# Decay rows sent straight to DRAM, sums left in their banks, and side work respaced in a decay-attention and two-FFN kernel

## The chip, the cores and the metric

One core of a Trainium2 chip runs the whole program in one launch. The metric is the device time of that launch in microseconds; of the timed runs the median counts. The engines are TensorE (PE in the profile; its weight loads PEld), VectorE (DVE), ScalarE (ACT), GpSimd (POOL) and SyncE (SP), which here only issues DMAs. Each works through its own queue in order.

## What is computed

Attention of 32 heads (4 batches of 8, 576 positions, head size 64) with a causal mask and a decay, then two feed-forward layers over 2304 tokens (512 to 2048 to 512), all in float32:

```python
scores = scale * np.matmul(q, k.transpose(0, 1, 3, 2))
log_f = np.log(np.clip(f, 0.0001, 1.0))
cum = np.cumsum(log_f, axis=-1)
decay = cum[:, :, :, None] - cum[:, :, None, :]
scores = np.where(causal, -1e9, scores + decay)
attn = softmax(scores)                       # written out in the reference
x = np.matmul(attn, v)                       # heads side by side: 2304 x 512
h = x @ w_in;  x = (h * np.clip(h + 3.0, 0.0, 6.0) / 6.0) @ w_out       # first layer
h = x @ w_in2; out = (np.maximum(h, 0) + alpha * np.minimum(h, 0)) @ w_out2   # second layer
```

## The kernel before

**Precision.** A float32 value is split into a high part (a cast, `fp32r`) and a low part (the value minus the cast), and a product is made of three matmuls: high by high, high by low, low by high. So each operand needs a cast on ACT and a subtraction on POOL or DVE.

**Attention** (lines 278 to 605) runs in 144 units, nine for each pair of heads: four query blocks of the first head, one tail unit for both, four blocks of the second. Unit t's scores are made at step t, the exps one step on, transposes and evacuation (`evac`, L408, L413) five steps on, into `pt` tiles. The decay is added by the matmul itself: rows 64 to 67 of the operands q2 and k2 hold the cumulated logarithms `hl` (high and low part) and constants. For heads 0 and 1 `aug_rows` copies these rows from SBUF; for the others all rows are written to DRAM once (`aq_d`, `ak_d`; L520, L536) and `prep_head` fetches four rows for each head (L313, L314). `aq` is a tile in which POOL has scaled `hl` by 1 (L531 to 534) beside memset constants. `load_head` (L295) loads a head's q and k. Head 2 is prepared at unit 3 and first used at unit 9. The tiles of the prologue (pool `pro`: fl, zero, cum, ak, aq) are given up behind it, and the pool of the `pt` tiles is opened in their place.

**The FFNs** work in sets of (layer, group g of 256 hidden columns, pair p of 768 tokens). For each set the first product is done as seven block products (Strassen-Winograd; `product`, L689): products 1, 6, 7, 4 add up in PSUM bank A, 5 and 3 in C, 2 in B. Partial sums are copied to SBUF tiles `s` by ACT (`keep`, L705) and added on DVE (`add`, L708); each sum is activated (`activate`: `first` on ACT L663 or L666 and L668, `second` on DVE L674 or L677, `third` a cast L682 on ACT and the low part L683 on POOL, the tile `g`), and the set after it multiplies g by w_out (`piece`, L731, L733). The order is written out: `SEQ` gives one step for each product (a digit) and each piece (`q`), 15 steps a set in the first layer and 13 in the second; `later(d, fn)` puts work d steps on.

**Side work** is put at steps by tables of names and step numbers (`conversion`, `build`). `conv_ops` turns 64-bit weights into float32 words (m on ACT L137; f, s, j, g on DVE L140 to L153; raw words come by `fetch`, L117), sums them (S1 to S4, POOL L167) and splits them (h on ACT L181, l on POOL L185). For four groups of the second layer the float32 words are made early and kept in DRAM (c, p: store and load, L195, L197); `CONV_TURN` is their table. `build` makes the seven X blocks of a pair: adds (a, L237), casts (h, ACT L240), subtractions (l, L245, in turn on the engines of `subs`). The third pair's blocks are built in the set (g 7, p 0) of each layer, by the list `BUILD`; pair 1 of the second layer in the last set of the first. A tile of a pool has as many buffers as it says; a new use waits for the readers of the old one.

Of the kernel before, what the change touches and what calls it, by code (L numbers as in the profile page):

```python
# [21 lines left out]
def decay_attention_ffn2_kernel(ctx, tc, qk, v, f, wi1, wo1, wi2, wo2, alpha, out):  # L22
# [22 lines left out]
    DRAIN = {9 * NP + 3: 2, 9 * NP + 4: 2, 9 * NP + 6: 2, 9 * NP + 7: 2}  # L45
    CONV_ATT = "m0 15 f0 16 s0 17 j0 18 g0 19 m1 24 f1 25 s1 26 j1 27 g1 28 hb 33 lb 35 S1 42 S3 42 S2 44 S4 44 ha 51 la 53 hc 53 lc 60 hd 60 ld 62 m2 69 f2 70 s2 71 j2 72 g2 73 m3 78 f3 79 s3 80 j3 81 g3 82 ho0 78 lo0 80 ho1 87 lo1 89 wi0 90 wi1 93 wo0 99 wo1 102"
    CONV_ATT1 = "m0 108 f0 109 s0 110 j0 111 g0 112 m1 117 f1 118 s1 119 j1 120 g1 121 S1 143 S3 145 S2 146 ha 146 hc 146 hb 147 la 147 lc 147 lb 148 S4 149 hd 149 ld 150 m2 150 f2 151 s2 151 j2 152 g2 153"
# [3 lines left out]
    CONV_EVEN = "m0 0 f0 1 s0 2 j0 3.5 g0 5 m1 4 f1 6.5 s1 8 j1 9 g1 10 S1 11 S2 12 S3 12 hc 13 ha 13 lc 14 hb 14 la 15 lb 16 S4 17 m2 18 hd 18 f2 19 ld 19 s2 20 j2 21 m3 21 g2 22.5 f3 23 ho0 23 lo0 24 s3 24.5 j3 26 g3 27 ho1 28 lo1 29 wi0 40 wi1 43 wo0 46 wo1 48"  # L51
    CONV_TURN = "p0 0 p1 0 S1 6 S2 7 S3 7 hc 8 ha 8 lc 9 hb 9 la 10 lb 11 S4 12 hd 13 ld 14 p2 14 p3 15 ho0 24 lo0 25 ho1 26 lo1 27 wi0 40 wi1 43 wo0 46 wo1 48"
    BUILD_FIRST = "h0 l0 a3 h3 l3 h2 l2 a4 a6 h6 l6 h4 l4 h1 l1 a5 h5 l5"
    BUILD = "h0 2 l0 4 a3 6 h3 9 l3 11 h2 9 l2 11 a4 13 a6 15 h4 16 l4 18 h1 17 l1 19 h6 19 l6 21 a5 22 h5 26 l5 28"
    early = {}
# [200 lines left out]

    def build_ops(k, p, add, subs, even=None):
        adds, highs, lows = build_parts(k, p, add, subs)
        if even is not None:
            fns = [{"h": highs, "l": lows, "a": adds}[name[0]][int(name[1]), c]  # L260
                   for name in BUILD_FIRST.split() for c in range(KH)]
            return [(even[0] + i / even[1], fn) for i, fn in enumerate(fns)]
        return [(t, {"h": highs, "l": lows, "a": adds}[name[0]][int(name[1]), c])
                for name, t in table(BUILD) for c in range(KH)]

# [12 lines left out]
    def attention():  # L278
        with ExitStack() as ax:
# [207 lines left out]
            def aug_rows(a):  # L487
# [50 lines left out]
            px.close()
# [115 lines left out]
    def activate(s, gt, i, n, h, d):  # L654
        ff, g, p = s
        if n not in gt:
            gt[n] = {}
        hold = {}

        def first():  # L660
            t = P["tp"].tile([128, NB], F32, tag="t", name="t")
            if ff == 0:
                nc.scalar.activation(out=t, in_=h(), func=AF.Relu, bias=three, scale=1.0)  # L663
                hold["g"] = t
                return
# [13 lines left out]

        def third():  # L680
            gt[n][i] = P["gp"].tile([128, 2, NB], F32R, tag=f"g{n}", name=f"g{n}", bufs=3 - n)
            nc.scalar.copy(out=gt[n][i][:, 0], in_=hold["g"])  # L682
            nc.gpsimd.tensor_sub(out=gt[n][i][:, 1], in0=hold["g"], in1=gt[n][i][:, 0].bitcast(F32))  # L683

        later(d, first)
        later(d + 1, second)
        later(d + 1, third)

    def product(s, c, gt, k):  # L689
# [67 lines left out]
    def side_work(s):  # L757
# [7 lines left out]

        def build(k, pair, subs, add=nc.vector, even=None):
# [17 lines left out]
        if p == NPR - 1:  # L784
# [118 lines left out]
```

## Time and profile before

| | us |
|---|---|
| median of 3 runs | 1015.56 (1013.59 to 1016.53) |
| profiled execution | 1012.13 |
| its span | 1010.3 |
| PE busy in the span | 965.5 |
| DVE, ACT, POOL busy | 735.9, 589.1, 590.0 |
| mean granted TensorE clock | 0.995 |

The profile is one execution, recorded by the hardware. Attention fills the span up to about 215 us, the first layer goes on to about 625, the second to the end. Matmuls are pipelined and their ends are modelled, so a PE that is always busy need not be at its peak; a gap in it is a real gap. A mark `[3.86 <-DMA k<-ak_d]` behind a row means that the engine sat idle for 3.86 us before it and that this DMA ended the idle time. The granted clock is a share of 2.4 GHz.

### The profile page before, as it was taken

The page shows a single profiled execution, that of the slowest core. Times are in us where ns is not written, and L with a number is a line of the kernel's source. Part 1 is how long each engine was busy: PE and PEld are TensorE (multiplying, and loading weights), DVE is VectorE, ACT ScalarE, POOL GpSimd, SP SyncE. Part 2 cuts the span into 40 slices and gives each one's busy share as a digit, 9 for nine tenths or more (in the row PEclk, how much of TensorE's full clock was granted, in tenths as well). Part 3 has the DMA queues.
Part 4 walks back from the last instruction along what each step waited for, and adds up shares of the span by engine and source line. Part 5 has one row for each costly group of instructions (what it writes and reads, how often), then busy time and mean ns, then how long its engine had stood idle before and what let it go on. Part 6 is the DMA issues. An engine that isn't in the chain of part 4 may idle for free.

```text
span 1010.3 us, 15919 instructions
## 1 busy us (share of the span) xinstructions
PE 965.5 (96%) x5488; PEld 859.7 (85%) x5488; DVE 735.9 (73%) x1284; ACT 589.1 (58%) x1444; POOL 590.0 (58%) x577
## 2 busy tenths in 40 slices
PE   4999999999999999999999989999999999999998
PEld 3767666678899999998998988789898888898997
DVE  6888988857698788878989846145687788735454
ACT  5677787776555555555654445665565656564452
POOL 8567568956646666566485269566556556532222
PEclk9999999999999999999999999999999999999999
DMA  6555576501424444310576851332344420243531
GB/s 219 174 173 168 176 239 208 150 2 42 156 66 177 178 175 169 107 48 1 198 308 241 308 184 48 137 129 81 125 160 168 166 84 1 104 182 142 229 150 68
DMA packets 36868, 147.57 MB, mean 146 GB/s; under 512 B 4668, under 2 KB 4668, under 8 KB 33652
## 3 DMA queue, kind: packets, MB, share of 16 engines
q1 hardware_dynamic: 36784, 146.56, 41.7%
q8 instruction: 43, 0.70, 0.3%
q14 instruction: 37, 0.30, 0.1%
q10 hardware_dynamic: 4, 0.00, 0.0%
HBM read 98.26 MB, written 44.14 MB: 141 GB/s over the span
## 4 chain that ended last, share of the span: by engine, by line
PE 57%; DVE 23%; POOL 7%; ACT 6%; issue 4%; DMA 2%; SPq 0%; POOLq 0%; ACTq 0%; DVEq 0%
PE o L733 13%; PE hA L700 12%; PE o L731 12%; PE hC L700 7%; PE pv L454 4%; PE hB L700 3%; DVE nm L341 3%; PE tp L397 2%; DVE t L674 2%; PE sc L364 2%; POOL wi L185 2%; POOL g L683 1%; DVE r L751 1%; DVE s L708 1%; ACT g L682 1%
## 5 line engine op out<-in xcount | busy, mean ns | idle before, releaser
L731 PE MATMUL o<-g,wo 128*128 128x384 f32 x1152 | 233.3, 341 | 2.0 <-POOL g L683 2.0
L700 PE MATMUL hA<-xh,wi 128*128 128x384 f32 x768 | 225.8, 339 | 9.0 <-ACT s L705 5.4
L733 PE MATMUL o<-wo,g 128*128 128x512 f32 x864 | 225.5, 395 | 4.0 <-POOL g L683 3.0
L683 POOL TENSOR_TENSOR g<-t,g 128x384 fp32r<-128x384 f32 x120 | 128.8, 1073 | 156.1 <-ACT g L682 134.6
L731 PEld LDWEIGHTS o<-g,wo 128*128 128x128 f32 x1152 | 205.6, 189 | 4.6 <-POOL g L683 3.3
L733 PEld LDWEIGHTS o<-wo,g 128*128 128x128 f32 x864 | 159.8, 188 | 33.2 <-POOL g L683 6.2
L683 POOL TENSOR_TENSOR g<-s,g 128x384 fp32r<-128x384 f32 x72 | 74.7, 1038 | 155.6 <-ACT g L682 153.8
L700 PEld LDWEIGHTS hA<-xh,wi 128*128 128x128 f32 x768 | 142.0, 188 | 15.1 <-ACT s L705 7.6
L751 DVE TENSOR_TENSOR r<-o,r 128x512 f32<-128x512 f32 x126 | 86.2, 687 | 73.8 <-PE o L733 73.7
L700 PE MATMUL hA<-xl,wi 128*128 128x384 f32 x384 | 129.7, 338 | 0.0
L682 ACT CAST g<-t 128x384 fp32r<-128x384 f32 x120 | 61.9, 515 | 113.0 <-DVE t L674 97.3
L700 PE MATMUL hC<-xh,wi 128*128 128x384 f32 x384 | 115.0, 340 | 3.6 <-ACT s L705 3.6
L740 DVE SCALAR_TENSOR_TENSOR r<-o,r 128x384 f32<-128x384 f32 x168 | 90.6, 549 | 21.2 <-PE o L731 21.0
L349 ACT ACTIVATE p<-sc,nm 128x128 f32<-128x128 f32 (+4 forms) x160 | 84.6, 532 | 22.9 <-DVE nm L341 10.9
L245 POOL TENSOR_TENSOR xl<-r,xh 128x384 fp32r<-128x384 f32 x65 | 78.5, 1225 | 4.1 <-ACT xh L240 3.7
L341 DVE TENSOR_REDUCE nm<-sc 128x1 f32<-128x128 f32 (+4 forms) x160 | 71.7, 470 | 10.1 <-PE sc L366 8.5
L700 PEld LDWEIGHTS hC<-xh,wi 128*128 128x128 f32 x384 | 71.3, 189 | 6.7 <-ACT s L705 4.6
L700 PEld LDWEIGHTS hA<-xl,wi 128*128 128x128 f32 x384 | 72.4, 189 | 3.1
L682 ACT CAST g<-s 128x384 fp32r<-128x384 f32 x72 | 37.1, 515 | 60.1 <-DVE s L677 53.4
L397 PE MATMUL tp<-ident,p 128*128 128x128 f32 x384 | 68.6, 282 | 0.6 <-ACT pt L413 0.6
L364 PE MATMUL sc<-k,q 128*128 128x256 f32 (+2 forms) x128 | 55.6, 434 | 11.9 <-DVE k L332 9.8
L700 PE MATMUL hC<-xl,wi 128*128 128x384 f32 x192 | 65.1, 339 | 0.0
(128 smaller groups left out, 1901.8 us busy)
## 6 DMA issues: line engine op xcount, KB each, us to landing
wid<-wi SPq DMA_DIRECT2D x24, 896.0 KB
wi<-wid SPq DMA_DIRECT2D x12, 1792.0 KB
rqk<-in_qk SPq DMA_DIRECT2D x32, 608.0 KB
raw<-in_wi SPq DMA_DIRECT2D x32, 512.0 KB
raw<-in_wo SPq DMA_DIRECT2D x32, 512.0 KB
wod<-wo SPq DMA_DIRECT2D x24, 512.0 KB
wo<-wod SPq DMA_DIRECT2D x12, 1024.0 KB
vt<-in_v SPq DMA_DIRECT2D x16, 320.0 KB
```

Of the source, the lines that this page charges most:

```text
L245: e.tensor_sub(out=XS[k][1][:, b, c], in0=x, in1=XS[k][0][:, b, c].bitcast(F32))
L341: nc.vector.tensor_reduce(out=nm[:, i:i + 1], in_=src, axis=AX.X, op=ALU.max, negate=True)
L349: nc.scalar.activation(out=pt[:, c0:c0 + cw], in_=src, func=AF.Exp, bias=nm[:, 0:1], scale=1.0, accum_out=dsts[i])
L364: nc.tensor.matmul(out=sc[:, 0:n], lhsT=q1[:, qs], rhs=k1[:, 0:n], start=True, stop=False)
L397: nc.tensor.transpose(tp[:, j, :], pt[:, 128 * j:128 * j + 128], ident)
L682: nc.scalar.copy(out=gt[n][i][:, 0], in_=hold["g"])
L683: nc.gpsimd.tensor_sub(out=gt[n][i][:, 1], in0=hold["g"], in1=gt[n][i][:, 0].bitcast(F32))
L700: nc.tensor.matmul(out=h, lhsT=a, rhs=b[:, x, kc], start=new and kc + e == 0, stop=kc == KH - 1 and e == 2, skip_group_check=not new)
L731: nc.tensor.matmul(out=o[:, 0:NB], lhsT=a[:, cs], rhs=b, start=st, stop=sp)
L733: nc.tensor.matmul(out=o, lhsT=b[:, cs], rhs=a, start=st, stop=sp)
L740: later(0, lambda: nc.vector.scalar_tensor_tensor(out=acc, in0=o[:, 0:NB], scalar=1.0 / 6.0, in1=acc, op0=ALU.mult, op1=ALU.add))
L751: nc.vector.tensor_add(out=acc, in0=o, in1=acc)
```

## The change

It has five parts. (1) Decay rows: the constants of `aq_d` come from a small memset tile early on, and the rows themselves are sent to DRAM straight from `hl`, ahead of `ak_d` and of `load_head(3)`; POOL's scaled copies go; the preparation of head 1 moves behind the masks; the first two weight fetches move from unit 2 to units 13 and 18, and the first block's conversion with them. (2) The sums of products 2 and 3 are written back into their PSUM bank and read there; only 7's goes to SBUF. (3) The second layer's activation is written as h + (1 - alpha) * relu(-h), one ACTIVATE instead of two. (4) All builds use one list `BUILD_FIRST`, with adds further ahead of the casts, at a fixed number of instructions a step; the third pair's adds go from DVE to POOL, and its subtractions alternate between DVE and POOL. (5) In `CONV_TURN` the sums come a step earlier and the casts up to four steps later.

```diff
-    CONV_ATT = "m0 15 f0 16 s0 17 j0 18 g0 19 m1 24 f1 25 s1 26 j1 27 g1 28 hb 33 lb 35 S1 42 ...
+    CONV_ATT = "m0 20 f0 21 s0 22 j0 23 g0 24 m1 26 f1 27 s1 28 j1 29 g1 30 hb 34 lb 35 S1 42 ...
-    CONV_TURN = "p0 0 p1 0 S1 6 S2 7 S3 7 hc 8 ha 8 lc 9 hb 9 la 10 lb 11 S4 12 hd 13 ld 14 p2 14 p3 15 ho0 24 ...
-    BUILD_FIRST = "h0 l0 a3 h3 l3 h2 l2 a4 a6 h6 l6 h4 l4 h1 l1 a5 h5 l5"
-    BUILD = "h0 2 l0 4 a3 6 h3 9 l3 11 h2 9 l2 11 a4 13 a6 15 h4 16 l4 18 h1 17 l1 19 h6 19 l6 21 a5 22 h5 26 l5 28"
+    CONV_TURN = "p0 0 p1 0 S1 5 S2 6 S3 7 hc 9.5 ha 10.5 lc 10.6 la 11.5 hb 12 lb 13 S4 14 hd 17 ld 18 p2 15 p3 18.5 ho0 24 ...
+    BUILD_FIRST = "h0 l0 a3 a4 h3 h2 l2 l3 a6 h4 l4 h1 h6 l1 a5 l6 h5 l5"
...
-            aq = pro.tile([NPP, 4, QW], F32R, name="aq")
+            aq = pro.tile([NPP, 2, QW], F32, name="aq")
             nc.gpsimd.memset(zero, 0.0)
+            nc.gpsimd.memset(aq, -1.0)
+            for a in range(2):
+                nc.gpsimd.memset(aq[32 * a:32 * a + 32, :, 576 - 64 * a:640 - 64 * a], 0.0)
...
             nc.sync.dma_start(out=alpha_sb, in_=alpha)
+            nc.sync.dma_start(out=aq_d.rearrange("a h r c -> (a h) r c")[:, 2:4], in_=aq)
+            for a in range(2):
+                nc.sync.dma_start(out=aq_d[a, :, 0:2, 576 - 64 * a:640 - 64 * a],
+                                  in_=zero[32 * a:32 * a + 32, 0:128].rearrange("p (r c) -> p r c", r=2))
...
-            nc.gpsimd.memset(aq.bitcast(F32)[:, :, 512:640], 0.0)
-            nc.gpsimd.memset(aq.bitcast(F32)[:, 2:4, 0:512], -1.0)
...
-            for a in range(2):
-                nc.gpsimd.memset(aq.bitcast(F32)[32 * a:32 * a + 32, 2:4, 512 + 64 * a:576 + 64 * a], -1.0)
             aug_rows(1)
             load_head(2)
+            nc.sync.dma_start(out=aq_d.rearrange("a h r c -> (a h) r c")[:, 0:2, 0:512], in_=hl[:, :, 0:512].bitcast(F32))
+            for a in range(2):
+                ps, t0 = slice(32 * a, 32 * a + 32), 512 + 64 * a
+                nc.sync.dma_start(out=aq_d[a, :, 0:2, t0:t0 + TAIL], in_=hl[ps, :, 512:S].bitcast(F32))
             for a in range(2):
                 nc.sync.dma_start(out=ak_d[a, 0:NP], in_=ak[32 * a:32 * a + NP].bitcast(F32))
             load_head(3)
-            prep_head(1)
-            prep_low(1)
...
-            scaled("P", aq[:, 0:2, 0:512], hl[:, :, 0:512].bitcast(F32))
-            for a in range(2):
-                ps, t0 = slice(32 * a, 32 * a + 32), 512 + 64 * a
-                scaled("P", aq[ps, 0:2, t0:t0 + TAIL], hl[ps, :, 512:S].bitcast(F32))
-            for a in range(2):
-                nc.sync.dma_start(out=aq_d[a, 0:NP], in_=aq[32 * a:32 * a + NP].bitcast(F32))
-            nc.gpsimd.tensor_scalar(out=alpha_sb, in0=alpha_sb, scalar1=-1.0, scalar2=None, op0=ALU.mult)
+            prep_head(1)
+            prep_low(1)
+            nc.gpsimd.tensor_scalar(out=alpha_sb, in0=alpha_sb, scalar1=-1.0, scalar2=1.0, op0=ALU.mult, op1=ALU.add)
...
-            aside(2, lambda: fetch(0), lambda: fetch(1))
+            aside(13, lambda: fetch(0))
+            aside(18, lambda: fetch(1))
...
             nc.scalar.activation(out=t, in_=h(), func=AF.Relu, scale=-1.0)
-            hold["g"] = g32 = P["tp"].tile([128, NB], F32, tag="t", name="t") if (i, n) == (1, 0) else h()
-            nc.scalar.activation(out=g32, in_=h(), func=AF.Relu)
-            hold["t"] = t
+            hold["g"] = t
...
-                nc.vector.scalar_tensor_tensor(out=g32, in0=hold["t"], scalar=alpha_sb[:, m:m + 1], in1=g32,
+                nc.vector.scalar_tensor_tensor(out=g32, in0=g32, scalar=alpha_sb[:, m:m + 1], in1=h(),
                                                op0=ALU.mult, op1=ALU.add)
...
         def add(k2):
-            nc.vector.tensor_add(out=c[k2], in0=h, in1=c[k2])
+            got = h if k != 7 else c[k2]
+            nc.vector.tensor_add(out=got, in0=h, in1=c[k2])
+            c[k2] = got
...
-            build(1, 1, both, even=(1, 1.5))
+            build(1, 1, both)
...
-                build(0, 1, (nc.gpsimd, nc.vector), nc.gpsimd)
+                build(0, 1, (nc.gpsimd, nc.vector), nc.gpsimd, (1, 1.35))
         if (g, p) == (NG - 1, 0):
-            build(1 if ff else 0, 2, both)
+            build(1 if ff else 0, 2, (nc.vector, nc.gpsimd), nc.gpsimd, (1, 1.5 if ff else 1.3))
```

## Rows read from the trace of the kernel before

**Rows 1.** The page, part 1: busy us, share of the span, instructions.

```profile
PE 965.5 (96%) x5488; PEld 859.7 (85%) x5488; DVE 735.9 (73%) x1284; ACT 589.1 (58%) x1444; POOL 590.0 (58%) x577
```

**Rows 2.** Waits of PE: engine, line, waited for, total us, times, longest.

```profile
PE hA L700 <- ACT s L705: 5.4, 6, 1.6
```

**Rows 3.** Timeline of PE: start, duration, instruction, idle time before it and releaser.

```profile
25.06 0.35 PE L365 MATMUL sc<-k,q 68*128 68x256 f32 x1 [3.86 <-DMA k<-ak_d]
...
243.26 0.44 PE L700 MATMUL hA<-xh,wi 128*128 128x384 f32 x1 [2.10 <-DVE s L708]
...
463.26 0.44 PE L700 MATMUL hA<-xh,wi 128*128 128x384 f32 x1 [1.62 <-ACT s L705]
...
598.49 0.46 PE L700 MATMUL hC<-xh,wi 128*128 128x384 f32 x1 [2.65 <-ACT s L705]
```

**Rows 4.** Windows: length; PE, PEld, DVE, ACT, POOL busy (x); clock, DMA, GB/s.

```profile
25.34:28.75 3.41, 3.41 (x16) 2.51 (x15) 1.82 (x7) 2.12 (x8) 0.95 (x2) 0.50 0.83 302
28.75:40.00 11.25, 11.25 (x92) 8.41 (x91) 9.46 (x19) 8.09 (x29) 5.81 (x6) 1.00 0.40 117
243.80:247.20 3.40, 3.40 (x13) 3.40 (x12) 3.12 (x6) 1.69 (x5) 1.43 (x2) 0.50 0.00 0
...
598.80:602.20 3.40, 3.40 (x12) 3.40 (x11) 1.24 (x3) 0.94 (x3) 3.32 (x4) 0.50 0.06 15
602.20:616.00 13.80, 13.80 (x79) 13.56 (x78) 9.26 (x15) 7.85 (x17) 11.59 (x12) 1.00 0.16 53
```

**Rows 5.** Windows over four stages, columns as in rows 4.

```profile
439.00:470.00 31.00, 28.75 (x161) 27.85 (x160) 28.27 (x43) 15.51 (x34) 20.35 (x17) 1.00 0.11 35
592.90:640.30 47.40, 40.16 (x205) 37.11 (x204) 22.40 (x36) 26.00 (x55) 44.33 (x42) 0.96 0.16 60
845.00:875.00 30.00, 27.92 (x135) 23.96 (x134) 25.75 (x37) 17.07 (x37) 18.85 (x16) 1.00 0.14 54
...
520.00:550.00 30.00, 28.05 (x151) 25.84 (x150) 27.46 (x41) 15.04 (x31) 21.68 (x19) 1.00 0.69 251
```

**Rows 6.** Timeline of SP's queue at the start: start, issue time, line, DMA.

```profile
12.24 0.84 SPq L520 DMA_DIRECT2D ak_d<-ak  x2
...
16.34 2.86 SPq L117 DMA_DIRECT2D raw<-in_wi  x2
```

**Rows 7.** Chain that ended last, in order of time: start, us, what.

```profile
14.56 5.79 DMA aq_d<-aq
20.73 4.20 DMA k<-ak_d
```

**Rows 8.** Timeline of ACT: the first evacuation, and two casts of cached weights.

```profile
17.52 0.27 ACT L408 COPY pt<-tp 128x128 f32<-128x128 f32 x1 [0.99 <-PE tp L397]
...
595.41 0.62 ACT L181 CAST wi<-wc 128x512 fp32r<-128x512 f32 x1 [5.37 <-POOL wc L167]
...
639.08 0.40 ACT L181 CAST wi<-wb 128x256 fp32r<-128x256 f32 x1 [4.16 <-POOL wb L167]
```

**Rows 9.** Tile t: duration ns min/median/max, first and last start, forms.

```profile
L674 DVE SCALAR_TENSOR_TENSOR t<-t,s x72: 544/552/1498, 222.0 to 610.1; 128x384 f32<-128x384 f32 x72
L674 DVE SCALAR_TENSOR_TENSOR t<-t,hA x24: 542/554/556, 230.0 to 612.0; 128x384 f32<-128x384 f32 x24
...
L668 ACT ACTIVATE t<-hA x24: 480/484/490, 629.8 to 999.2; 128x384 f32<-128x384 f32 x24
```

**Rows 10.** Lines by form: busy us, mean ns, idle us before and its releasers.

```profile
L245 POOL TENSOR_TENSOR xl<-r,xh 128x384 fp32r<-128x384 f32 x65 | 78.5, 1225 | 4.1 <-ACT xh L240 3.7
...
L237 POOL TENSOR_TENSOR r<-r 128x384 f32<-128x384 f32 x24 | 28.6, 1209 | 0.2
...
L708 DVE TENSOR_TENSOR s<-hC,s 128x384 f32<-128x384 f32 x48 | 26.6, 553 | 39.2 <-PE hC L700 27.2 <-ACT s L705 11.4 <-issue 0.3
...
L237 DVE TENSOR_TENSOR r<-r 128x384 f32<-128x384 f32 x24 | 22.9, 988 | 0.0
...
L245 DVE TENSOR_TENSOR xl<-r,xh 128x384 fp32r<-128x384 f32 x19 | 16.2, 865 | 7.3 <-ACT xh L240 7.3
```

More of the change, by code (lines that the diff above doesn't have):

```diff
@@ L45, in decay_attention_ffn2_kernel @@
     DRAIN = {9 * NP + 3: 2, 9 * NP + 4: 2, 9 * NP + 6: 2, 9 * NP + 7: 2}
-    CONV_ATT = "m0 15 f0 16 s0 17 j0 18 g0 19 m1 24 f1 25 s1 26 j1 27 g1 28 hb 33 lb 35 S1 42 S3 42 S2 44 S4 44 ha 51 la 53 hc 53 lc 60 hd 60 ld 62 m2 69 f2 70 s2 71 j2 72 g2 73 m3 78 f3 79 s3 80 j3 81 g3 82 ho0 78 lo0 80 ho1 87 lo1 89 wi0 90 wi1 93 wo0 99 wo1 102"
+    CONV_ATT = "m0 20 f0 21 s0 22 j0 23 g0 24 m1 26 f1 27 s1 28 j1 29 g1 30 hb 34 lb 35 S1 42 S3 42 S2 44 S4 44 ha 51 la 53 hc 53 lc 60 hd 60 ld 62 m2 69 f2 70 s2 71 j2 72 g2 73 m3 78 f3 79 s3 80 j3 81 g3 82 ho0 78 lo0 80 ho1 87 lo1 89 wi0 90 wi1 93 wo0 99 wo1 102"
     CONV_ATT1 = "m0 108 f0 109 s0 110 j0 111 g0 112 m1 117 f1 118 s1 119 j1 120 g1 121 S1 143 S3 145 S2 146 ha 146 hc 146 hb 147 la 147 lc 147 lb 148 S4 149 hd 149 ld 150 m2 150 f2 151 s2 151 j2 152 g2 153"
@@ L51, in decay_attention_ffn2_kernel @@
     CONV_EVEN = "m0 0 f0 1 s0 2 j0 3.5 g0 5 m1 4 f1 6.5 s1 8 j1 9 g1 10 S1 11 S2 12 S3 12 hc 13 ha 13 lc 14 hb 14 la 15 lb 16 S4 17 m2 18 hd 18 f2 19 ld 19 s2 20 j2 21 m3 21 g2 22.5 f3 23 ho0 23 lo0 24 s3 24.5 j3 26 g3 27 ho1 28 lo1 29 wi0 40 wi1 43 wo0 46 wo1 48"
-    CONV_TURN = "p0 0 p1 0 S1 6 S2 7 S3 7 hc 8 ha 8 lc 9 hb 9 la 10 lb 11 S4 12 hd 13 ld 14 p2 14 p3 15 ho0 24 lo0 25 ho1 26 lo1 27 wi0 40 wi1 43 wo0 46 wo1 48"
-    BUILD_FIRST = "h0 l0 a3 h3 l3 h2 l2 a4 a6 h6 l6 h4 l4 h1 l1 a5 h5 l5"
-    BUILD = "h0 2 l0 4 a3 6 h3 9 l3 11 h2 9 l2 11 a4 13 a6 15 h4 16 l4 18 h1 17 l1 19 h6 19 l6 21 a5 22 h5 26 l5 28"
+    CONV_TURN = "p0 0 p1 0 S1 5 S2 6 S3 7 hc 9.5 ha 10.5 lc 10.6 la 11.5 hb 12 lb 13 S4 14 hd 17 ld 18 p2 15 p3 18.5 ho0 24 lo0 25 ho1 26 lo1 27 wi0 40 wi1 43 wo0 46 wo1 48"
+    BUILD_FIRST = "h0 l0 a3 a4 h3 h2 l2 l3 a6 h4 l4 h1 h6 l1 a5 l6 h5 l5"
     early = {}
@@ L255, in build_parts, with build_ops @@
         return adds, highs, lows
-    def build_ops(k, p, add, subs, even=None):
+    def build_ops(k, p, add, subs, even):
         adds, highs, lows = build_parts(k, p, add, subs)
[L259 to L264, printed above, removed]
+        fns = [{"h": highs, "l": lows, "a": adds}[name[0]][int(name[1]), c]
+               for name in BUILD_FIRST.split() for c in range(KH)]
+        return [(even[0] + i / even[1], fn) for i, fn in enumerate(fns)]
     def x_places(c, t0, t1):
@@ L764, in conversion, with build @@
                     aside(t * scale + shift, ops[name])
-        def build(k, pair, subs, add=nc.vector, even=None):
+        def build(k, pair, subs, add=nc.vector, even=(1, 1.5)):
             for t, fn in build_ops(k, pair, add, subs, even):
```

## Prediction

> **What bounds the kernel now.** I read the busy times first: PE is busy for 965.5 of 1010.3 us, DVE for 735.9, ACT and POOL for about 590 each [rows 1]. So PE sets the end, and no edit here takes a matmul away: all there is to win is PE's 45 us of idle time, and what its clock loses behind it. The list of PE's waits says whom it waits for: behind the wait for the first scores the largest sum is bank A waiting for the copy of L705 on ACT, six times, 5.4 us [rows 2]. PE's own timeline places the four largest waits after the start-up: 3.86 us before 25.06, 2.10 before 243.26, 1.62 before 463.26, 2.65 before 598.49 [rows 3]. Then the clock: three stretches of 3.4 us stand at a granted 0.50, that is at 1.2 GHz instead of 2.4, each right behind one of these waits (3.86, 2.10 and 2.65 us; none behind the 1.62). PE starts 16 matmuls in 3.41 us there (4.7 a us) and 92 in the next 11.25 (8.2 a us); 12 in 3.40 (3.5) against 79 in 13.80 (5.7) [rows 4]. Lost: 1 - 4.7/8.2 = 43% of 3.41 = 1.45 us, and 1 - 3.5/5.7 = 38% of 3.40 = 1.3 us. I take 1.4 us a stretch. Last, windows over the stages where the waits cluster show who is full there: DVE at 439 to 470 and 845 to 875, POOL at 593 to 640 [rows 5].
>
> **The change, part by part.**
>
> *Decay rows direct.* Unit 9 (pair 1) needs rows 64 to 67 of k2 of head 2. The chain: three POOL copies fill aq; its write to aq_d is issued at 14.56 and has landed 5.79 us later, behind the loads of heads 2 and 3; only then does SP issue q2 and k2 of head 2, and k2, issued at 20.73, lands 4.20 us later, because one megabyte of raw weights, issued from 16.34 on for 2.86 us, is ahead of it [rows 6, 7]. Both causes go: aq_d is now written straight from hl right behind load_head(2), where the writes of ak_d stood at 12.24, ahead of the load of head 3, and the two fetches go to units 13 and 18. New instructions: three DMAs of constants on SP early on (0.36 MB by the shapes), when SP has nothing else to issue until the decay rows are there; three DMAs of hl in place of two of aq, at 0.42 us each (two of ak_d took 0.84), so that ak_d and load_head(3) are issued about 1.3 us later. POOL loses three copies and three memsets and gains three memsets; preparing head 1 moves behind ident and maskj, and its first reader is the fifth unit, so that costs nothing unless POOL is over 2 us late. I expect aq_d and ak_d landed at 17.5 to 18.5 and k2 of head 2, behind head 3's load, at about 20.5 to 21, which is when PE gets there (25.06 - 3.86 = 21.2). One new wait: the pt tiles lie where fl to ak lay, so the first evacuation (ACT, 17.52) must wait until ak has been read, about 18.2 by the issues above: 0.7 us, and behind it on ACT stand the exps of the next units, for which PE's transposes wait [rows 8]. Sum: -3.86 - 1.45 + 0.7 = -4.6. Bounds: +0.5 (the rows are as late as before, ACT's wait comes on top) to -5.3. I stay near the full gain because the megabyte that the 4.20 us consist of is gone in any case.
> The first weight block's conversion starts five units later, with the same instructions; its first cast (hb) is still four units behind its last word operation, so I count nothing, and a step of ACT's waiting if that is too short.
>
> *Sums in banks, one ACTIVATE less.* For products 2 and 3 the add L708 writes its bank instead of s, and L663, L674 and L677 read PSUM. The trace has no DVE write to PSUM. The same add to SBUF (0.553) is the nearest row, the two-SBUF add L237 (0.988) the far one: 0 to 0.44 us each, 96 times, 0 to 42 us on a DVE that is idle for 274; below nothing isn't excluded, by some 0.1 each. I take the nearest, 0. The reader of the sum gains: L674 with t and s in SBUF has a median of 0.552 but a maximum of 1.498; with hA in PSUM all 24 lie within 0.542 to 0.556 [rows 9, 10]. So the 48 whose sum moves lose their long cases. The bank is now held until the STT, two steps after its product; bank C's next product, 5, comes nine to eleven steps after 3, so PE isn't touched while DVE lags less than seven steps. In the second FFN 96 ACTIVATEs of L668 (0.48 us) vanish: 46 us of ACT, and half a us of latency of each activation, both hidden under PE's matmuls except where PE waits for a g.
> The Trainium skill (SBUF — State Buffer, Who interferes with whom) says that a DVE instruction with two SBUF inputs and a GpSimd instruction that reads SBUF exclude each other for the whole length of the first. The 1.498 against 0.556 of L674 agrees. By this rule the adds that now go to GpSimd take back on DVE what they save there; rival (2) is what that would give.
>
> *Third pair.* Each of the two builds had 8 adds on DVE (0.988) and its 14 subtractions as 10 on POOL (1.225) and 4 on DVE (0.865); now 8 adds on POOL (1.209) and 7 subtractions on each [rows 10]. POOL: 8 x 1.209 - 3 x 1.225 = +6.0 us; DVE: -8 x 0.988 + 3 x 0.865 = -5.3. At 439 to 470 that makes POOL 20.35 + 6.0 = 26.4 of 31.0 and DVE 28.27 - 5.3 = 23.0; at 845 to 875 POOL 18.85 + 6.0 = 24.9 of 30, DVE 25.75 - 5.3 = 20.5 [rows 5]. Both fit. A cast of xh waits on ACT for an add that now stands three steps or more ahead of it, so the copy of L705 no longer stands behind that wait. PE's idle time there is 2.25 and 2.08 us; I take 1.4 and 1.5 away. Bounds: +2 each (POOL's g late) to the whole idle time.
>
> *Order of the other builds.* Before 243.26 DVE works off a backlog; ahead of the add that PE awaits there the new order puts two adds more (2 x 0.988) and takes one subtraction (0.865) and one blocked L674 (up to 0.94) away: nothing gained, the 2.10 us and their clock stay. The adds that leave the queue behind it give -0.4. Bounds +1.5 to -4.5. At 520 to 550 PE idles for 30 - 28.05 = 1.95 us [rows 5], mostly behind blocked L674s: -0.8, between 0 and -1.95.
>
> *The turn, 593 to 640.* ACT stands 5.37 us for the sums of the cached weights (until 595.41) and 4.16 us (until 639.08), in order, with the copies of L705 behind it [rows 8]. Now the sums come a step earlier and the casts one to four steps later. p2 and p3 are issued on SP one and three steps later; their readers (ho0, ho1) are still six steps off, and the stores behind them on SP are due twenty steps on: nothing. PE's idle time there is 47.40 - 40.16 = 7.24 us, plus 1.3 of clock. But POOL is busy for 44.33 of 47.40 [rows 5], and no instruction is taken off it: if POOL sets the stage, 3.1 us is all. Two adds and a subtraction more even come ahead of the g's with which the second FFN begins. So the wait at 598 shrinks, PE is earlier, and meets POOL's late g. I take -3.0; bounds +1 to -8.5.
>
> **Sum:** -4.6 - 0.4 - 1.4 - 0.8 - 3.0 - 1.5 = -11.7 us. The profiled execution took 1012.13 (span 1010.3): 1000.4. The median of the runs is 1015.56, 3.4 above it; from that, 1003.9.
>
> **Rivals.** (1) *The wait at 25 us only changes its name:* the rows queue behind head 3's load, or ACT's new wait is longer. For it: three more DMAs stand ahead of ak_d, and SP and the DMA queue keep their order. Against: the megabyte is gone. Price 4.6: 1008.5. 12%. (2) *GpSimd's adds block DVE* for up to their own length: 8 x 1.209 = 9.7 us on DVE's 23.0 of 31 make 32.7, so both third-pair stages keep their idle time (2.9) and grow by 1.7 each: 1010.2. For it the 1.498 of L674; against it that its median is 0.552, so most meet no block. 10%. (3) *Slower: GpSimd falls behind at the third pairs,* and PE's pieces wait for g, whose low part (L683) stands behind the adds in the same queue. It decides once POOL's 26.4 us exceed 31: if its some 25 instructions there take 0.19 us more each. Then its 6.0 us fall on PE twice, each with 1.4 of clock: +14.8; the turn, where POOL is fullest, gives nothing; left are -4.6 - 0.4 - 0.8: 1015.56 + 9.0 = 1024.6. 8%. (4) *ACT was the turn's only limit,* and the backlog at 241 goes too: 5.5 more there, 3.5 more here: 994.9. 14%. (5) *Nothing reaches PE:* the waits are those of another queue: 1015. 6%. My forecast, 1000 to 1008: 50%.
>
> **How the numbers follow.** A measurement of this kernel can tell about 0.3%, 3 us. Faster by more: the forecast, (1), (2), (4) = 0.86, less 0.02 for the upper end of (2): 0.84. Within: (5) and that 0.02: 0.08. Slower: (3): 0.08. The range takes in the forecast, (1), (2) and the near half of (4): 50 + 12 + 10 + 7 = 79%, 996.5 to 1010.5.
>
> **What would show it.** No PE wait at 21 to 25 us and a full clock from there on; ACT's first evacuation waiting for a DMA at about 18; L674 and L677 of products 2 and 3 never above 0.65 us; POOL 6 us fuller and DVE 5 us emptier in both third-pair stages, PE's idle time under 1 us; at the turn ACT's waits for POOL's sums under 2 us, POOL still above 90%. I am wrong if PE's total idle time falls by under 5 us, if PE waits for L683 for over 8 us in sum, or if hB or hC wait for an STT.

## The result and the profile after

The changed kernel takes 1001.09 us (median, 999.62 to 1002.92) against 1014.58 of the kernel before beside it: ratio 0.9867, 95% interval 0.9839 to 0.9895, 13.5 us less. The forecast was 1003.9, by a sum of -11.7. The total is near by luck, its composition is not right: what I had put at zero gains most, the largest of my terms nearly vanishes, and part of the change costs time.

The profiled execution took 1002.92, its span is 1000.9. The page's busy line of it, to be read beside [rows 1]:

```profile
PE 966.4 (97%) x5488; PEld 864.5 (86%) x5488; DVE 713.4 (71%) x1274; ACT 540.6 (54%) x1348; POOL 590.4 (59%) x583
```

PE's work is the same, its idle time fell from 44.8 to 34.5 us. PE's timeline with the largest waits that are left behind the first scores, and ACT's at the two places where it explains them; columns as in [rows 3]:

```profile
19.72 0.69 PE L360 MATMUL sc<-k,q 128*128 128x384 f32 x1 [1.68 <-ACT p L345]
53.95 0.58 PE L374 MATMUL sc<-k,q 68*128 68x288 f32 x1 [2.60 <-DVE pt L404]
256.31 0.44 PE L696 MATMUL hA<-xl,wi 128*128 128x384 f32 x1 [2.35 <-POOL xl L244]
258.00 0.44 PE L696 MATMUL hA<-xl,wi 128*128 128x384 f32 x1 [0.89 <-DVE xl L244]
597.39 0.69 PE L696 MATMUL hC<-xh,wi 128*128 128x384 f32 x1 [3.20 <-ACT s L701]
```
```profile
18.91 0.27 ACT L404 COPY pt<-tp 128x128 f32<-128x128 f32 x1 [3.89 <-DMA ak_d<-ak]
594.71 0.62 ACT L180 CAST wi<-wc 128x512 fp32r<-128x512 f32 x1 [6.35 <-POOL wc L166]
```

Of the four waits of [rows 3] three are gone (25.06, 243.26 down to 0.49, 463.26); the one at the turn grew from 2.65 to 3.20, and those at 19.7, 54 and 256 are new. Windows of stages (columns as in [rows 4, 5]); the first two stand behind new waits, the third begins in the last microsecond of the turn's wait, and the last four answer to [rows 5], moved with the work where PE is earlier:

```profile
53.70:60.53 6.83, 6.58 (x32) 5.24 (x32) 2.90 (x8) 3.26 (x13) 2.89 (x4) 0.50 0.61 203
258.50:261.90 3.40, 3.40 (x12) 3.40 (x11) 2.07 (x4) 1.30 (x3) 1.97 (x2) 0.50 0.44 153
596.40:603.25 6.85, 5.86 (x18) 5.86 (x19) 2.51 (x6) 3.56 (x8) 6.85 (x7) 0.50 0.00 0
...
440.00:471.00 31.00, 31.00 (x178) 31.00 (x177) 25.37 (x44) 17.99 (x38) 24.85 (x24) 1.00 0.10 35
520.00:550.00 30.00, 29.30 (x165) 28.52 (x164) 27.77 (x45) 15.13 (x32) 20.66 (x18) 1.00 0.75 270
592.00:637.00 45.00, 40.88 (x207) 38.72 (x206) 23.88 (x38) 25.27 (x54) 43.57 (x42) 0.92 0.23 86
837.00:867.00 30.00, 29.94 (x148) 26.57 (x147) 23.02 (x35) 15.67 (x35) 26.59 (x24) 1.00 0.15 56
```

The third-pair stages have lost all of PE's idle time but 0.06 us; the one at 520 still has 0.70 us of 1.95, the turn 4.1.

PE's instructions stand in the same order in both kernels, so the start of the same matmul can be compared. The table gives, for each stretch (times of the kernel before), how much earlier (-) the changed kernel is at its end than at its beginning, and the same for kernels with one part of the change alone (the experiments below):

| stretch | forecast | changed | single parts |
|---|---|---|---|
| start to 227 | -4.6 | +1.8 | rows 0.0 |
| 227 to 269 | -0.4 | +1.2 | banks and ACTIVATE -0.4 |
| 269 to 474 | -1.4 | -3.0 | third pair -2.2, banks and ACTIVATE -1.2 |
| 474 to 557 | -0.8 | -2.4 | banks and ACTIVATE -1.7 |
| 557 to 649 | -3.0 | -1.9 | turn -1.4 |
| 649 to 880 | -1.5 | -4.9 | ACTIVATE alone -4.9, third pair -1.0 |
| sum | -11.7 | -9.3 | |

The terms are rounded. The sum is 9.3 and not 13.5 because these are two single executions, 1012.13 and 1002.92; the first stretch also holds how late the first scores began: 9.8 to 11.2 us in kernels with the old prologue, 8.6 to 9.0 with the new one. One execution tells that stretch only to some 2 us: up to 227 three kernels below (a1_oldlist, a3_words, b1_words) run the code of the changed kernel and stand at -0.7, -0.6 and +3.1 there. Others repeat well: the changed kernel and all its variants lie at -3.0 from 269 to 474, and at -4.8 to -4.9 from 649 to 880.

### The profile page after: what moved, and what is told of

The parts are those of the page before. It is cut to its first block, busy times and chain, and to the rows that moved or that the text cites. A ratio compares the mean times of both kernels' runs of the same rounds, so it can differ in the third digit from the quotient of the medians.

```text
span 1000.9 us, 15848 instructions
## 1 busy us (share of the span) xinstructions
PE 966.4 (97%) x5488; PEld 864.5 (86%) x5488; DVE 713.4 (71%) x1274; ACT 540.6 (54%) x1348; POOL 590.4 (59%) x583
## 4 chain that ended last, share of the span: by engine, by line
PE 71%; DVE 14%; POOL 5%; issue 3%; ACT 3%; DMA 3%; SPq 1%; ACTq 0%; DVEq 0%; POOLq 0%
PE o L731 19%; PE hA L696 16%; PE o L729 13%; PE hC L696 8%; PE pv L450 4%; PE hB L696 4%; DVE nm L337 3%; PE tp L393 2%; PE sc L360 2%; POOL g L679 1%; DVE t L670 1%; PE sc L361 1%; DVE nm L339 1%; POOL r L236 1%; DMA fd<-wa 1%
## 5 line engine op out<-in xcount | busy, mean ns | idle before, releaser
L679 POOL TENSOR_TENSOR g<-t,g 128x384 fp32r<-128x384 f32 x192 | 202.7, 1056 | 287.1 <-ACT g L678 268.9
L678 ACT CAST g<-t 128x384 fp32r<-128x384 f32 x192 | 98.7, 514 | 188.8 <-DVE t L673 92.5
L244 POOL TENSOR_TENSOR xl<-r,xh 128x384 fp32r<-128x384 f32 x59 | 68.5, 1174 | 3.8 <-ACT xh L239 3.6
L701 ACT COPY s<-hA 128x384 f32<-128x384 f32 x96 | 45.8, 477 | 36.6 <-PE hA L696 36.3
L696 PE MATMUL hB<-xh,wi 128*128 128x384 f32 x192 | 57.1, 338 | 0.0
```

What stands on the lines that cost most here:

```text
L244: e.tensor_sub(out=XS[k][1][:, b, c], in0=x, in1=XS[k][0][:, b, c].bitcast(F32))
L696: nc.tensor.matmul(out=h, lhsT=a, rhs=b[:, x, kc], start=new and kc + e == 0, stop=kc == KH - 1 and e == 2, skip_group_check=not new)
```

## The parts alone

Each part was put alone into the kernel before, with the lines of the diff above: p1_rows has part 1 (the prologue's hunks, the fetches, `CONV_ATT`), p2_banks parts 2 and 3 (`add`, `first`, `second`, the scale of alpha), p4_turn the new `CONV_TURN` and the build of pair 1 in the last set with the new list at (1, 1.35). In p3_third `build` takes its list as an argument (`NEW` is the new one), and only the third pair's two builds change:

```diff
-            build(1 if ff else 0, 2, both)
+            build(1 if ff else 0, 2, (nc.vector, nc.gpsimd), nc.gpsimd, (1, 1.5 if ff else 1.3), NEW)
```

> Kernel before (1014.6) with part 1 alone: decay rows sent straight from hl, fetches at units 13 and 18, first block's conversion five units later; adds, activations and builds as before. Theory: the wait of 3.86 us at 25 us goes, but this part brings the wait of 2.60 us at 54 us with 6.8 us of half clock that the changed kernel shows, since the fetches now stand on SP right ahead of head 7's rows; net +1 to +2 us, 1015 to 1017, with a PE wait of 2 to 3 us at 53 to 56 us. Rival, my prediction's step: -4.6 us, 1010, no PE wait over 1 us behind 30 us.

> Kernel before with parts 2 and 3 alone: sums of products 2 and 3 left in their bank, one ACTIVATE in the second layer. Theory by my prediction's step: 0, so 1013 to 1016; the add keeps its 0.55 us, no STT of products 2 and 3 above 0.65 us, PE's waits stay where they are. Rival: the gains of the changed kernel that lie above my terms (1.5 us more at 520 to 550, 3.3 us more at 785 to 875) are this part's, through the blocked STTs that go and ACT's 46 us: about -5, so 1009.5, with PE's lead growing over the whole second layer.

> Kernel before with the third pair's two builds alone in the new form: adds on GpSimd, the new list, 1.3 and 1.5 instructions a step. Theory: both stages lose their PE idle time, 2.0 to 3.0 us each as in the changed kernel's first stage, -4 to -6, so 1009 to 1010.5. Rival A: DVE has room only if the sums in banks are there too; then -1 to -2, about 1013. Rival B, GpSimd's adds hold DVE up: no gain, 1014.6, with DVE's instructions in these stages longer than before.

> Kernel before with the turn alone: the new table of the cached words, and the new list and spacing for the first block of the second layer. Theory: the start of the turn is set by the load of the cached words (issued at about 588, landed at about 592), so the PE wait at 598 stays at 2 to 3.5 us and its half clock too; the later ACT wait of 4.16 us goes, and with it 1 to 2 us: 1012.5 to 1013.5. Rival, my prediction's step: the wait at 598 shrinks to under 1.5 us, -3.0: 1011.6.

| kernel | ratio to before | 95% interval | us | forecast |
|---|---|---|---|---|
| p1_rows | 0.9991 | 0.9979 to 1.0003 | -0.9 | -4.6 |
| p2_banks | 0.9908 | 0.9890 to 0.9926 | -9.3 | 0 |
| p3_third | 0.9965 | 0.9949 to 0.9980 | -3.5 | -2.9 |
| p4_turn | 0.9973 | 0.9960 to 0.9986 | -2.7 | -3.0 |

*p1_rows* bears the theory out in kind: the wait at 25 goes and one at 55 comes. Its interval holds 1, so that neither the small loss of the theory nor a gain is shown. PE is 3.1 us ahead at 43.6 us, then it stands at the tail unit. PE's row and SP's queue ahead of it:

```profile
55.06 0.37 PE L378 MATMUL sc<-k,q 68*128 68x288 f32 x1 [3.45 <-DMA k<-k]
```
```profile
40.54 0.47 SPq L326 DMA_DIRECT2D k<-k  x1
45.16 0.36 SPq L117 DMA_DIRECT2D raw<-in_wo  x1
45.61 0.28 SPq L313 DMA_DIRECT2D q<-aq_d  x1
45.94 0.29 SPq L314 DMA_DIRECT2D k<-ak_d  x1
46.28 0.74 SPq L295 DMA_DIRECT2D rqk<-in_qk  x1
47.11 0.38 SPq L300 DMA_DIRECT2D vt<-in_v  x1
47.59 0.47 SPq L326 DMA_DIRECT2D k<-k  x1
```

The fetch of raw words stands in SP's queue for DVE's sign step, 4.1 us by SP's waits, and what SP then issues, 1.44 MB in 2.3 us, goes out just ahead of the 144 KB copy of head 7's k rows. That copy, issued at 47.59, ends PE's wait at 55.06. In the changed kernel's own trace the same wait bears the name of an evacuation on DVE, which ended 0.15 us ahead of it; in p1_rows, a1_oldlist, a3_words, b1_words and b3_ak that of this copy. The Trainium skill (DMA: Bandwidth & Descriptors, Queues, rings and completion order) says that DMAs issued by one queue share its rings and are taken in ring order; the trace agrees: from the issue of this copy, behind 1.44 MB, to the end of PE's wait for it are 7.5 us.

*p2_banks* speaks for the rival and gives nearly twice as much. *p3_third* gains what I forecast, at 465 (-1.9) and behind 860 (-1.5); its interval, -2.0 to -5.2 us, does not exclude the theory's -4. Its windows, to be read beside [rows 5]:

```profile
439.00:470.00 31.00, 30.72 (x174) 30.16 (x173) 26.01 (x42) 17.46 (x37) 24.93 (x24) 1.00 0.10 35
845.00:875.00 30.00, 28.57 (x141) 25.06 (x141) 24.28 (x34) 18.16 (x40) 27.01 (x24) 1.00 0.14 54
```

PE's idle time falls from 2.25 to 0.28 us in the first stage, without any sum in a bank, so rival A does not hold there; in the second it only falls from 2.08 to 1.43. *p4_turn*: PE's wait stays (3.34 us at 598.94), and the gain comes after it, as its theory said; its interval, -1.4 to -4.1 us, takes in the theory's amount and the rival's. The half clock that the theory expected did not come in this execution (last section).

Whether p2's gain is the bank's or the ACTIVATE's was split by the single ACTIVATE alone (the STT reads t and s, both in SBUF):

```diff
-            hold["g"] = g32 = P["tp"].tile(...) if (i, n) == (1, 0) else h()
-            nc.scalar.activation(out=g32, in_=h(), func=AF.Relu)
-            hold["t"] = t
+            hold["g"] = t
...
-                ... in0=hold["t"], scalar=alpha_sb[:, m:m + 1], in1=g32,
+                ... in0=g32, scalar=alpha_sb[:, m:m + 1], in1=h(),
```

> Kernel before (1014.6, 1013.8 beside the first four experiments) with the single ACTIVATE of the second layer alone; all sums stay in s. It splits the 9.3 us that banks and ACTIVATE together gave. Theory: what counts is that the STT finds one operand in PSUM; in the second layer s is still in SBUF here, so the blocked STTs stay and only ACT's 46 us go: 0 to -2 us, 1012 to 1014. Rival: the gain of the second layer (lead of PE from 2.7 us at 597 to 8 us at 868) is the vanished ACTIVATE's, half a us of latency in each chain: -4 to -5.5, about 1009, with PE's lead starting behind 615 us.

It took 0.9943 (0.9929 to 0.9956) of the kernel before, -5.8 us: the rival, except that PE's lead begins only at 780, not at 615. So of the 9.3 us some 5.8 are the ACTIVATE's and, by the difference, 3.5 the banks', which fall in the first layer. The traces say the same: from 227 to 649 p2_banks gains 3.5 us and p5_act none, from 649 to 880 they gain 4.6 and 4.9. Two windows of p5_act; the second has the place of the third in [rows 5]:

```profile
785.00:825.00 40.00, 40.00 (x200) 36.05 (x200) 34.27 (x57) 19.96 (x42) 22.04 (x21) 1.00 0.38 138
845.00:875.00 30.00, 30.00 (x150) 26.72 (x149) 26.77 (x39) 15.37 (x34) 19.90 (x18) 1.00 0.16 62
```

PE starts 150 matmuls in the 30 us where it started 135, 11% more, although it had been idle for 7% only. Compared over the same 470 matmuls (780 to 880 of the kernel before), p5_act is 4.9 us faster, where PE had been idle for 2.8. In the second layer g is the stationary operand of the pieces (L733 `o<-wo,g`), so a late g also holds up weight loads, and such stalls are not all shown as idle time of PE. The waits of PEld from 780 to 880, two rows of the kernel before (ten waits, 6.3 us) and the one of p5_act (columns as in [rows 2]):

```profile
PEld o L733 <- POOL g L683: 4.3, 6, 1.2
PEld o L733 <- ACT g L682: 2.0, 4, 0.9
...
PEld o L731 <- POOL g L681: 0.4, 1, 0.4
```

## The waits that the change brought

Edits of the changed kernel at four places, each taking away what one wait was put down to. The times are compared through their ratios to the kernel before (0.9867 for the changed kernel). That ratio is itself known only to 2.8 us, so by the times alone the gain of b2_fetch is clear of noise, that of b1_words just so, and those of a1_oldlist and b3_ak are not.

**The wait at 256.** The old list, for pair 1 of slot 1 only:

```diff
-            build(1, 1, both)
+            build(1, 1, both, names="h0 l0 a3 h3 l3 h2 l2 a4 a6 h6 l6 h4 l4 h1 l1 a5 h5 l5")
```

> The changed kernel (1001.1) with the old list of build steps for pair 1 of slot 1 alone (in the new list the low part of block 6 comes at places 30 and 31 of 36 instead of 20 and 21). Theory: PE's waits for xl of 2.35 and 0.89 us at 256 to 258 go and the 3.4 us of half clock behind them, while the old wait for the add at 243 (2.1 us and clock) comes back only if the list, not the sums in banks, had taken it away: -3 to -5 us, 996 to 998. Rival: the waits only move back to 243, 1000 to 1001.

0.9853 (0.9833 to 0.9872); median 998.93. Both waits for xl are gone; 1.31 us at 241.66 and 1.90 at 261.65 come back. From 227 to 269 PE gains 0.9 where the changed kernel loses 1.2: 2.1 us by the traces, 1.4 by the ratios, less than expected, and the times alone would not tell it from nothing. The loss repeats in the traces of the five other kernels with the new list there: +0.9 to +2.0 (a2_fetch, a3_words, b1_words, b2_fetch, b3_ak). The new list puts the low part of block 6 at places 30 and 31 of 36, and product 6 is the third of its set.

**The wait at 54.** First the sign steps, and so the fetches, at units 27 and 32; then the fetches taken out of the sign step:

```diff
-    CONV_ATT = "m0 20 f0 21 s0 22 j0 23 g0 24 m1 26 f1 27 s1 28 j1 29 g1 30 hb 34 ...
+    CONV_ATT = "m0 20 f0 21 s0 22 j0 23 g0 27 m1 26 f1 27 s1 28 j1 29 g1 32 hb 34 ...
```
```diff
-            fetch(wseq.index((ff, g, s)) + 2)
+            if (ff, g, s) not in wseq[0:2]:
+                fetch(wseq.index((ff, g, s)) + 2)
...
+            aside(28, lambda: fetch(2))
+            aside(37, lambda: fetch(3))
```

> The changed kernel (1001.1) with the sign steps of the first block's words, and with them the two fetches that follow them on SP, at units 27 and 32 instead of 24 and 30, behind the copies of heads 7 and 8. Theory: the wait of 2.6 us at 54 us is the copy of head 7's k rows, landing behind 1.4 MB of weights, q, k and v that SP issued in one go after it had stood 3.7 us for the sign step; with the fetch behind that copy the wait falls under 0.7 us and the 6.8 us of half clock go: -3 to -5, 996 to 998. Rival: the wait is that of the DVE evacuation which the trace names, and stays: 1001.

> The changed kernel (1001.1) with the fetches of the third and fourth weight words taken out of the sign step and put on SP behind the copies of heads 7 and 9, at units 28 and 37, where the sign steps they wait for are long done. Theory: a2_fetch only moved the wait by one pair (2.15 us at 67, again the copy of k rows, of head 9, behind a fetch that held SP up); without a fetch that waits ahead of a head's loads there is no PE wait over 0.7 us between 30 and 100 us and no half clock there: -2.5 to -4.5, 996.5 to 998.5. Rival: the DMA rings are full there whatever the order, the wait comes again one pair on: 1000 to 1001.

a2_fetch: 0.9863 (0.9846 to 0.9880), no gain. The wait at 54 is gone, and one comes again one pair later, behind the next fetch; its row names no releaser. PE and SP of a2_fetch:

```profile
67.34 0.37 PE L374 MATMUL sc<-k,q 68*128 68x288 f32 x1 [2.15 <-issue]
```
```profile
58.03 0.38 SPq L116 DMA_DIRECT2D raw<-in_wo  x1
...
59.18 0.36 SPq L291 DMA_DIRECT2D rqk<-in_qk  x1
60.59 0.36 SPq L296 DMA_DIRECT2D vt<-in_v  x1
61.04 0.49 SPq L322 DMA_DIRECT2D k<-k  x1
```

b2_fetch: 0.9826 (0.9813 to 0.9840), -4.2 us against the changed kernel: no wait for the copy of a head's k rows is left. The same bytes are moved, so full rings are not the cause by themselves. The edit takes away two things at once, a fetch that waits in SP's queue ahead of a head's loads, and its 512 KB ahead of the copy; which of them counts more is not shown.

**The wait at 19.7.** Two tiles of the prologue change places:

```diff
-            ak = pro.tile([NPP, 4, S], F32R, name="ak")
             aq = pro.tile([NPP, 2, QW], F32, name="aq")
+            ak = pro.tile([NPP, 4, S], F32R, name="ak")
```

> The changed kernel (1001.1) with two tiles of the prologue in exchanged places: aq ahead of ak, so that the first pt tile lies on fl, zero, cum and aq, and no longer on ak. Theory: ACT's first evacuation (18.91, 3.89 us of waiting) waits for ak only because it is written where ak lay; now it starts at 16 to 17.5, PE's wait of 1.68 us at 19.7 goes, and the clock is full 1 to 2 us earlier: -1 to -2.5, 998.5 to 1000, unless it is lost again at 54. Rival: the wait is for the transposes or another transfer, and ACT's first evacuation stays at 18.5 to 19: 1001.

0.9841 (0.9820 to 0.9862), -2.6. ACT's first evacuation now starts 3.1 us earlier and waits for a cast on POOL only:

```profile
15.77 0.27 ACT L404 COPY pt<-tp 128x128 f32<-128x128 f32 x1 [0.99 <-POOL k L91]
```

PE's 1.68 us are gone. So ACT had waited only because the first pt tile lay on ak. What that is worth in the end is not shown: -2.6 is within the noise, and the same matmul that starts at 50 us in the kernel before comes 3.5 us earlier in b3_ak, and 2.5 to 4.1 us earlier in the changed kernel and the five variants that keep the tiles' order (a1_oldlist, a2_fetch, a3_words, b1_words, b2_fetch).

**The turn.** The cached words were loaded earlier. The diff is that of b1_words; a3_words puts both loads at 6 * 14 + 5, the second waiting for a store, and the load of the next wi six steps later:

```diff
-                    tag = ("wa", "wb", "wc")[(4 * g + s) % 3]
+                    tag = ("wc", "wa", "wb")[(4 * g + s) % 3]
...
+                    if k == 14:
+                        early["turn"] = conv_ops(1, 0)
+                        aside(6 * k + 2, early["turn"]["p0"])
+                    if k == 15:
+                        aside(6 * k + 5, early["turn"]["p1"])
...
-                conversion(conv_ops(1, 0), CONV_TURN, True, 1, 7)
+                conversion(early["turn"], CONV_TURN, True, 1, 7, 1)
```

> The changed kernel (1001.1) with the cached words of the turn loaded some 10 us earlier: the tiles of the caching turn by one place, so that the first two words need not wait for the last store, and the 1.8 MB load of the next wi goes behind that store. Theory: at 592 POOL and ACT stood 6.9 and 6.4 us for this load, and PE's 3.2 us at 597 with 6.8 us of half clock come from it: -4 to -6, 995 to 997, ACT's wait for POOL's sums under 2 us. Rival: POOL is full from 592 to 637 whatever the load does, PE then meets its late low parts: 0 to -2, 999 to 1001.

> The changed kernel (1001.1) with the turn's words loaded earlier as before, but the 1.8 MB load of the next wi left in its place: the first word's load goes 9 steps ahead, the second right behind the store of the last cached words, without waiting for that store to land. Theory: both are there some 4 us earlier than 592, POOL's first sum starts at 585 to 588, ACT's 6.4 us fall under 3 and PE's 3.2 us at 597 under 1.5, with its half clock: -3 to -5, 996 to 998, and no wait for wi. Rival: PE only meets POOL's late work further on in the turn (a3_words regained 3 us before 602 and kept none of it beyond what its wait for wi took): 0 to -1, 1000 to 1001.

a3_words: 0.9868 (0.9848 to 0.9887), no gain. POOL's first sum starts at 585.06, but I had put the next wi's load behind the stores, and PE waits for that:

```profile
589.32 0.69 PE L696 MATMUL hA<-xh,wi 128*128 128x384 f32 x1 [5.39 <-DMA wi<-wid]
```

It decides nothing. b1_words, without that: 0.9831 (0.9810 to 0.9853), -3.7. POOL's first sum in b1_words, to be read beside the changed kernel's (the second fence):

```profile
589.06 0.73 POOL L166 TENSOR_TENSOR wc<-wa,wb 128x256 f32<-128x256 f32 x1 [2.91 <-DMA wb<-fd]
```
```profile
592.29 0.73 POOL L166 TENSOR_TENSOR wc<-wa,wb 128x256 f32<-128x256 f32 x1 [6.94 <-issue]
```

POOL starts 3.2 us earlier, ACT waits 2.33 us in place of 6.35, PE's wait of 3.20 is gone (1.53 for a g at 606 is new). From 557 to 649 b1_words gains 5.8 us on the kernel before, the changed kernel, a1_oldlist, a2_fetch, b2_fetch and b3_ak 1.3 to 2.5. So the turn's first wait was a DMA's: the load of the first word had to follow the store of the last, and that store stood behind 2.8 MB of weights (SP stands 7.5 us for it).

**All four together:**

> The changed kernel with four of the experiments' edits together: the old list of build steps for pair 1 of slot 1, the words of the turn loaded earlier, the fetches at units 28 and 37, aq ahead of ak. Their ratios to the kernel before were 0.9853, 0.9831, 0.9826 and 0.9841 against 0.9867 for the changed kernel. Theory: the four waits stand in four places that do not feed each other, so the gains add up: 0.9867 - 0.0014 - 0.0036 - 0.0041 - 0.0026 = 0.975, some 990 us. Rival: they are partly the same microseconds, an earlier PE meets other engines' work still undone; then the best of the four is nearly all, 0.981 to 0.983, 996 us.

991.94 us, 0.9769 (0.9755 to 0.9784) of the kernel before, 23 us less, faster than both. Of the 11.9 us that the ratios add up to, 9.9 came: additive as far as their noise of some 3 us tells.

## Why the prediction was right, and where not

*Decay rows, forecast -4.6, measured -0.9, not clear of noise.* The wait for head 2's rows went, and ACT's new wait for ak came, at 18.91, not 18.2. There I was too cheap, and rival (1) half right: 0.7 us was the delay of one copy, while PE stood 1.68 us for it. What this costs in the end is not shown (b3_ak).

The step that failed is "so I count nothing" for the first block's conversion. I looked at its casts on ACT, and not at the fetches tied to its sign steps: the first moves from unit 19 to 24, right ahead of the loads that SP issues at unit 25. b2_fetch prices that at 4.2 us; with the 0.9 that is 5.1, near my 4.6.

One reading under my 4.6 was wrong as well, that the megabyte of weights is what "the 4.20 us consist of". In the kernel with all four edits PE is early enough to meet head 2's rows again; the copy is issued at 17.32, with the weights behind it, and still takes over 4 us. What brought the rows forward is their earlier issue (17.32 against 20.73). SP and PE of that kernel:

```profile
17.32 0.24 SPq L311 DMA_DIRECT2D k<-ak_d  x1
...
22.66 0.43 SPq L116 DMA_DIRECT2D raw<-in_wi  x1
```
```profile
21.64 0.36 PE L362 MATMUL sc<-k,q 68*128 68x256 f32 x1 [1.39 <-DMA k<-ak_d]
```

(The part also takes four memsets off POOL, not three; no term rests on that.)

*Sums in banks and one ACTIVATE less, forecast 0, measured -9.3.* The add costs the same, as the nearest row said, and the STTs (scalar_tensor_tensor, on DVE) of products 2 and 3 have lost their long cases:

```profile
L705 DVE TENSOR_TENSOR hC<-hC,s x48: 549/566/567, 224.5 to 981.6; 128x384 f32<-128x384 f32 x48
L670 DVE SCALAR_TENSOR_TENSOR t<-t,hB x24: 535/542/555, 223.7 to 610.6; 128x384 f32<-128x384 f32 x24
L670 DVE SCALAR_TENSOR_TENSOR t<-t,hC x24: 540/546/555, 226.8 to 603.1; 128x384 f32<-128x384 f32 x24
L670 DVE SCALAR_TENSOR_TENSOR t<-t,s x24: 545/930/1372, 228.5 to 607.2; 128x384 f32<-128x384 f32 x24
```

All this was forecast, but no time was set against it. The failing step is "both hidden under PE's matmuls except where PE waits for a g": I never priced the exception. PE's timeline of the kernel before shows six waits for a g between 790 and 874, 2.8 us in sum, of which this is the longest:

```profile
855.99 1.19 PE L733 MATMUL o<-wo,g 128*128 128x512 f32 x4 [0.72 <-POOL g L683]
```

I had given that stage's idle time to the third pair alone, which takes 0.65 us of it when it stands alone. What makes g earlier, the half us of latency or the emptier ACT, these runs don't separate. For the banks' 3.5 us my sum has only the -0.8 at 520, under another part: that shorter STTs reach PE in the first layer was not priced either.

*Third pair, forecast -2.9, measured -3.5.* Right, on a sum that is partly wrong. At 439 to 470 of p3_third POOL is busy for 24.93 us (forecast 26.4), DVE for 26.01, not 23.0. In part that is work that an earlier PE draws into the window (two more STTs, two more adds of L708), in part the STTs with both inputs in SBUF take longer, 0.921 us (6 of them) in place of 0.642 (4). Their group in that stretch of p3_third (line, shapes, count | busy us, mean ns | idle before):

```profile
L674 DVE SCALAR_TENSOR_TENSOR t<-t,s 128x384 f32<-128x384 f32 x6 | 5.5, 921 | 1.5 <-ACT t L663 1.4
```

This is the mechanism of rival (2). The Trainium skill (SBUF — State Buffer, Who interferes with whom) has such an instruction and a GpSimd read exclude each other; the trace agrees, in the changed kernel too, where the 24 STTs that still read t and s have a median of 0.930 against 0.552 before [rows 9] (there of three products; in p2_banks, with the old builds, the same 24 have 0.559). It costs PE nothing there, because DVE has 5 us of room.

*Order of the builds, forecast -0.4 and -0.8.* The first is a loss of 1.4 to 2.1 (a1_oldlist; by the traces rather than by the times): I counted which adds stand ahead of DVE's late one, and not when each block is due. The gain at 520 to 550 came, 2.4 us; 1.7 of it is the banks', and the rest belongs to no part that was run alone.

*The turn, forecast -3.0, measured -2.7.* The later waits went (the 4.16 us of ACT [rows 8]), the one I had wanted to shrink did not. I followed PE's wait to ACT's, ACT's to POOL's, and stopped. POOL's own row of before has idle time ahead of its first sum, for which no engine is named:

```profile
592.96 0.74 POOL L167 TENSOR_TENSOR wc<-wa,wb 128x256 f32<-128x256 f32 x1 [3.88 <-issue]
```

POOL had nothing to start earlier with, and moving the sum a step ahead only set it in front of a low part.

*The sum.* The parts alone make -0.9 - 9.3 - 3.5 - 2.7 = -16.4; with the list's +1.4 to +2.1 some -14.5, against -13.5 measured; banks and third pair both take from the waits at 457 to 463 (1.2 and 2.2 us alone, 3.0 together), and from 649 to 880 the third pair adds nothing to what the ACTIVATE gives (1.0 and 4.9 alone, 4.9 together). That I came out near, at -11.7, is luck: losses of 5 to 6 us that I had not seen (rows, list) stand against 9 us that I had put at nothing. The signs of being wrong that I had named did not show: PE's idle time fell by 10 us, its waits for L679 (L683 before) are 2.4 us in sum, and nothing of PE waits for an STT. But two of the signs of being right failed: at the turn ACT waits 6.35 us for POOL's sums, not under 2, and in the third-pair stages DVE is 2.9 and 2.7 us emptier, not 5.

## What to carry to other kernels

A wait is followed until its chain reaches work or a transfer that could not have started earlier; a queue that stands idle ahead of the releaser means that the chain goes on, here into a DMA and its issue order. When a step is moved, each DMA tied to it is placed against what stands behind it in its queue, above all when it must itself wait. And each "hidden except where PE waits for it" is priced at once from the list of PE's waits.

## Not expected of the hardware

After PE's waits of 2.60 and 3.20 us the granted clock stood at 0.50, 1.2 GHz, for 6.8 us, twice the stretches of [rows 4]. The length of the wait does not tell: behind 3.45 us in p1_rows (at 55) and 3.67 in p2_banks (at 596) it stood at 0.50 for 3.4 us, behind 2.45 in a1_oldlist (at 52) for 6.8, and behind 3.34 in p4_turn not at all. PE's wait in p4_turn and the window behind it:

```profile
598.94 0.44 PE L700 MATMUL hC<-xh,wi 128*128 128x384 f32 x1 [3.34 <-ACT s L705]
```
```profile
599.00:606.00 7.00, 6.70 (x37) 6.38 (x38) 2.58 (x6) 3.25 (x7) 7.00 (x7) 1.00 0.00 0
```

Nor does the code: behind the same wait of 2.1 us at 243 to 245, reached by the same instructions, the kernel before has such a stretch [rows 4], p3_third, p4_turn and p5_act have none; behind the wait at 54 the changed kernel and a1_oldlist have 6.8 us, a3_words 3.4. This is part of why single traces of the same code differ by some us. In 53.70 to 60.53 of the changed kernel PE started 32 matmuls; in the kernel with all four edits, with no such wait, 56 in the same stretch of time:

```profile
53.70:60.50 6.80, 6.80 (x56) 4.46 (x55) 4.87 (x10) 4.61 (x18) 5.31 (x5) 1.00 0.43 133
```

By these two rates (not quite the same matmuls) 43% of 6.83 us, an estimated 2.9 us, went to the clock, as much as the wait itself, where I had taken 1.4 a stretch.
